# Logits with keys innermost, weighted values with keys outermost, the attention residual put into the accumulation bank, and a written-out instruction sequence

## The chip, the cores and the metric

The kernel runs on one core of one Trainium2 chip. The metric is the time of one execution on the device in microseconds (us), the median of several runs. The core has five engines that run side by side, each through its own list of instructions in order: TensorE (PE; its weight loader is a row of its own, PEld), VectorE (DVE), ScalarE (ACT), GpSimd (POOL) and SyncE (SP), which issues most DMAs. An engine that comes to an instruction whose input isn't there, or whose destination is still in use, waits, and everything behind it in its list waits too. The order of these five lists is therefore a large part of what this kernel is.

## The reference

One block of a transformer on 2048 rows of 640 numbers, in float32: a layer norm, attention in 32 heads of 20 over 8 keys each (the row itself and those 2, 4, ... 14 rows before it), the output projection and a residual; then a second layer norm, a gated feed-forward of width 1728 and a second residual.

```python
q, k, v = heads(layernorm(x) @ wqkv)              # 32 heads of 20
idx = pos[:, None] - 2 * arange(8)                # 8 keys a row, dilation 2
logits = einsum("bhsd,bhswd->bhsw", q, k[idx]) * 20 ** -0.5     # masked where idx < 0
o = einsum("bhsw,bhswd->bhsd", softmax(logits), v[idx])
h = x + o @ wo
n = layernorm(h)
out = h + (silu(n @ w_gate) * (n @ w_up)) @ w_down
```

## The kernel before, in words

**Tiling.** The rows are worked in four batches of 512 (`b`, NB = 4), each as four row blocks of 128 (`j`, NJ = 4). The heads are worked in four groups of eight (`g`, NG = 4, 160 columns). The normalized rows of a batch are turned into columns (transposes L604 for batch 0; by way of VectorE and DRAM for the others) and multiplied with the weights. To keep float32 accuracy each operand is split in two parts (a cast by ScalarE, a subtraction by VectorE), and each product is made of three passes over the parts; so 15 matmuls (three passes, five blocks of 128 columns) make one row block's product. The names are: `x` rows and their columns in `sha` (even batches) or `shb` (odd ones); the K, Q, V weights, loaded at L616 and split at L617 and L619; the products in `bank`s of PSUM (L643), taken out by ScalarE (L648) and stored in DRAM (`ksc`, `qsc`, `vsc`).

**Attention.** For each batch and group, two halves `jp` of two row blocks: VectorE multiplies the query with its eight keys (L692, 2560 elements a partition), sums over the 20 numbers of a head (L699, 128 results), takes the largest over the keys (L706 to L711), ScalarE takes the exponent, VectorE sums (L721), scales, multiplies with the values (L727, 2560) and adds the eight weighted values by halving (L735, L741, and GpSimd in some groups). Within a row block the logits lie key by key, eight heads side by side ("j w h"), and so do the weighted values.

**Output projection** (`wo`, L838). The attention's result comes back in columns (splits L879 and L880), and for each row block `j` and each half of the 640 output columns 15 matmuls of 320 columns accumulate in one bank (L890). ScalarE copies the bank into a scratch row (`XN`, L893), and VectorE adds the scratch row to the residual: in place in the row `h` of batches 1 to 3 (L896, loaded ahead with `x`), or with a freshly loaded row of `x` in batch 0 (L901). Then come the row's statistics (L389 and others), its normalization, the transposes (L504, splits L506 and L507 for a pair of row blocks) and the feed-forward (gates and ups L962, downs L973 and others, with L986 and L990 reading the last gates' banks). The bank of a projection is the next of a list: banks 5, 6 and 7 in batch 0, bank 7 alone in batches 1 and 2, banks 7 and 4 in batch 3. These are the code's numbers; the order shows them as bank_73 to bank_75 for 5 to 7, bank_72 for 4 and bank_68 to bank_71 for 0 to 3.

**What sets the order.** Each piece of work is a call `P.add(engine, cost, function, reads, writes)`. A planner then runs through all of them with a table of costs, several rounds of due times (`ROUNDS`) and a table of corrections (`SHIFT`) to single pieces, and the pieces are issued in the order of the start times so found, as far as what they read and write allows. No bank, row or scratch is chosen by the planner: which bank a piece uses is fixed when it is added.

## Time and profile before

| what | value |
|---|---|
| time of one execution, three runs | 836.17, 837.33, 838.05 us; median 837.33 |
| profiled execution, first to last instruction (its span) | 835.3 us |
| TensorE busy, of the span | 826.3 us (99%) |
| TensorE's weight loader | 712.8 us (85%) |
| VectorE | 755.7 us (90%) |
| ScalarE | 421.3 us (50%) |
| GpSimd | 23.1 us (3%) |
| mean granted clock of TensorE | 0.999 |

The profile gives for the profiled execution its span alone, not a time as the runs have it. The span is 2.0 us under the median of the runs (837.33 - 835.3) and 0.9 under the shortest. In the lines of the profile a row has the engine, the line in the kernel, the operation, what it writes and reads, the shape as partitions x elements, and the times. Where a row ends in a bracket, the bracket tells how long the engine stood idle before it and for what. In the list of waits the three numbers are the sum in us, the count and the longest; in a row of groups they are the sum, the mean of one in ns, and the idle time just before them. A row of stretches has the engines in the order PE, PEld, DVE, ACT, POOL, SP with their busy time, then the granted clock, the busy share of the DMA engines and GB/s.

### The profile page before, as it was taken

To read this page: it belongs to the slowest core of one execution; us is meant where nothing else is said; L and a number is where in the kernel's file an instruction comes from. 1 tells how busy PE (TensorE), PEld (TensorE's weight loads), DVE (VectorE), ACT (ScalarE), POOL (GpSimd) and SP (SyncE) were. 2 spreads that over 40 slices of the span, in tenths; PEclk is the share of its full clock that TensorE was granted. 3 is DMA by queue.
4 is the path that set the end of the run, shared out by engine and by line. 5 is a ranking of instruction groups with operands and counts; after the bars stand their busy time and mean duration, and the time that the engine had idled before them with its cause. 6 is when DMAs were issued, how large, how long until landed. Compare 5 with 4: busy or idle time off the path is not lost.

```text
span 835.3 us, 11299 instructions
## 1 busy us (share of the span) xinstructions
PE 826.3 (99%) x4061; PEld 712.8 (85%) x4061; DVE 755.7 (90%) x916; ACT 421.3 (50%) x740; POOL 23.1 (3%) x34
## 2 busy tenths in 40 slices
PE   8999999999999999999999999999999999999998
PEld 6888888889978888887888888888988888888998
DVE  7599999999999999999999999998869888777982
ACT  7856473333783435654543476565695323323440
POOL 0000000000100000001000000000000000000000
PEclk9999999999999999999999999999999999999999
DMA  8897868568679764899899758899999634457722
GB/s 274 288 348 275 267 213 283 185 207 308 186 219 343 257 197 177 326 303 349 282 313 349 271 173 315 255 288 352 352 339 320 224 115 151 124 175 258 273 99 75
DMA packets 113223, 211.08 MB, mean 253 GB/s; under 512 B 37952, under 2 KB 70400, under 8 KB 112528
## 3 DMA queue, kind: packets, MB, share of 16 engines
q1 hardware_dynamic: 112864, 209.96, 74.0%
q8 instruction: 32, 0.52, 0.2%
q10 hardware_dynamic: 304, 0.41, 0.1%
q14 instruction: 23, 0.19, 0.1%
HBM read 151.27 MB, written 59.05 MB: 252 GB/s over the span
## 4 chain that ended last, share of the span: by engine, by line
PE 84%; DVE 8%; ACT 3%; DMA 3%; issue 1%; SPq 0%; POOL 0%; DVEq 0%; ACTq 0%; POOLq 0%
PE bank L962 22%; PE bank L1046 18%; PE bank L643 15%; PE bank L973 10%; PE bank L1298 7%; PE bank L890 6%; DMA fa<-in_x_dram 2%; PE bank L1103 1%; DVE fa L692 1%; PE bank L1093 1%; DVE fa L735 1%; PE bank L1068 1%; DVE fa L727 1%; DVE fa L699 1%; ACT ra L617 1%
## 5 line engine op out<-in xcount | busy, mean ns | idle before, releaser
L962 PE MATMUL bank<-shb,ra 128*128 128x512 f32 x810 | 190.0, 390 | 1.3 <-DVE shb L507 1.3
L962 PEld LDWEIGHTS bank<-shb,ra 128*128 128x128 f32 x810 | 151.4, 188 | 32.7 <-ACT shb L506 1.5
L643 PE MATMUL bank<-ra,sha 128*128 128x480 f32 x480 | 105.2, 379 | 0.2 <-ACT ra L617 0.2
L643 PE MATMUL bank<-ra,shb 128*128 128x480 f32 x470 | 102.5, 378 | 0.0
L643 PEld LDWEIGHTS bank<-ra,sha 128*128 128x128 f32 x480 | 89.8, 188 | 14.5 <-ACT ra L617 0.6
L643 PEld LDWEIGHTS bank<-ra,shb 128*128 128x128 f32 x470 | 88.1, 188 | 13.2
L692 DVE TENSOR_TENSOR fa<-fa 128x2560 f32<-128x2560 f32 x32 | 90.2, 2820 | 0.9 <-DMA fa<-qsc 0.4
L727 DVE TENSOR_TENSOR fa<-fa 128x2560 f32<-128x2560 f32 x32 | 90.3, 2822 | 0.8
L699 DVE TENSOR_REDUCE fa<-fa 128x128 f32<-128x2560 f32 x32 | 89.9, 2810 | 0.4
L1046 PE MATMUL bank<-shb,ra 128*128 128x512 f32 x360 | 89.4, 395 | 0.6 <-DVE fa L990 0.6
L973 PE MATMUL bank<-ra,acts 128*128 128x512 f32 x328 | 80.7, 391 | 0.0
L1046 PEld LDWEIGHTS bank<-shb,ra 128*128 128x128 f32 x360 | 66.0, 188 | 16.2 <-DVE fa L1223 1.7
L735 DVE TENSOR_TENSOR fa<-fa 128x1280 f32<-128x1280 f32 (+2 forms) x70 | 76.7, 1096 | 1.3
L890 PE MATMUL bank<-ra 128*128 128x320 f32 x480 | 74.1, 310 | 0.0
L890 PEld LDWEIGHTS bank<-ra 128*128 128x128 f32 x480 | 71.7, 188 | 2.4 <-ACT fa L893 1.0
L648 ACT ACTIVATE st<-bank,fa 128x480 f32<-128x480 f32 x64 | 41.0, 656 | 64.1 <-PE bank L643 59.5
L973 PEld LDWEIGHTS bank<-ra,acts 128*128 128x128 f32 x328 | 61.1, 188 | 13.2 <-DVE acts L997 0.5
L1046 PE MATMUL bank<-ra 128*128 128x512 f32 x288 | 69.1, 390 | 0.0
L1046 PEld LDWEIGHTS bank<-ra 128*128 128x128 f32 x288 | 53.9, 188 | 11.1
L1223 DVE TENSOR_TENSOR fa<-bank,fa 128x512 f32<-128x512 f32 x60 | 41.0, 689 | 19.8 <-PE bank L1046 19.0
L939 ACT CAST ra<-fa 128x1280 fp32r<-128x1280 f32 (+1 forms) x38 | 45.6, 1207 | 22.9 <-PE bank L962 12.3
L996 ACT CAST acts<-fa 128x512 fp32r<-128x512 f32 x34 | 21.0, 620 | 48.7 <-DVE fa L986 47.0
(189 smaller groups left out, 1059.8 us busy)
## 6 DMA issues: line engine op xcount, KB each, us to landing
fa<-in_ffn_dram SPq DMA_DIRECT2D x28, 960.0 KB, 6.4
fa<-ksc SPq DMA_DIRECT2D x16, 880.0 KB, 5.4
fa<-vsc SPq DMA_DIRECT2D x16, 880.0 KB, 7.3
ra<-lsc SPq DMA_DIRECT2D x21, 640.0 KB, 5.8
ra<-lsc SPq DMA_DIRECT2D x27, 320.0 KB, 3.7
lsc<-ra SPq DMA_DIRECT2D x13, 640.0 KB, 4.6
fa<-in_ffn_dram SPq DMA_DIRECT2D x12, 640.0 KB, 4.0
ra<-tsc SPq DMA_DIRECT2D x8, 960.0 KB, 7.1
```

The source lines that it names most:

```text
L643: T.matmul(banks[bk][:, 0:480], l, r_(wq(g, w, c), 480), start=(p, c) == first_mm, stop=(p, c) == last_mm)
L648: P.add("ACT", act(480) + 0.06, lambda bk=bk, j=j: A.activation(stage_t()[:, so : so + 1920].rearrange("p (t j c) -> p t j c", t=3, j=NJ)[ ...
L692: P.add("DVE", dve(2560), lambda: V.tensor_tensor(f(PROD, 2560).rearrange("p (j w c) -> p j w c", j=2, w=W), window(ko, 2 * jp), f(qo + 32 ...
L699: P.add("DVE", dve(2560), lambda: V.tensor_reduce(f(lo + 128 * jp, 128), f(PROD, 2560).rearrange("p (n d) -> p n d", d=DH), axis=AX.X, op= ...
L727: V.tensor_tensor(f(PROD, 2560).rearrange("p (j w d) -> p j w d", j=2, d=DH), bass.AP(tensor=fa[:, vo : vo + 160].tensor, offset=fa[:, vo ...
L735: V.tensor_add(dst(v), v[:, :, 0:m, :], v[:, :, m : 2 * m, :])
L890: T.matmul(banks[bk][:, 0:320], l, r_(m, 320), start=p == 0 and c == 0, stop=p == 2 and c == NC - 1)
L939: P.add("ACT", act(n), lambda: A.copy(r_(gu, n), f(raw, n)), r=[rf(raw, n)], w=[rr(gu, n)], prio=PR["fh"])
L962: T.matmul(banks[bk], r_(gu + 1280 * w + wid * c + col, 128), x2(a, c), start=p == 0 and c == 0, stop=p == 2 and c == NC - 1)
L973: T.matmul(banks[bk][:, lo:hi], l, m, start=first and p == 0, stop=last and p == len(passes) - 1)
L1046: T.matmul(banks[bk], r_(ws[w] + 256 * q, 128), x(a, c), start=start and p == n == q == 0, stop=stop and p == 2 and n == len(terms) - 1 an ...
L1298: T.matmul(banks[bks[j]][:, 0:320], t(a, 128, 128 * j), r_(ws[w], 320), start=p == q == 0, stop=p == NP - 1 and q == 2)
```

## The change

It has four parts.

1. The logits lie head by head, the eight keys of a head side by side ("j h w"); the largest and the sum over the keys read eight neighbours. The reduce that makes the logits now writes its 128 results in that order.
2. The weighted values lie key by key across both row blocks of the half ("w n d"), so that each halving is a sum of two stretches without gaps.
3. In batches 1 and 2, and in row blocks 2 and 3 of batch 0, ScalarE copies the residual row into the bank ahead of the output projection's matmuls (20 copies of 320 columns). The first matmul then adds to the bank instead of starting it; ScalarE's copy out of the bank writes the row `h` itself, and VectorE's ten additions (eight of L896, two of L901) are gone. Batch 3 and row blocks 0 and 1 of batch 0 stay as they were.
4. The planner, its costs, `ROUNDS` and `SHIFT` are gone. A table `ORDER` of all pieces, by number, takes their place. The transposes of L504 are issued as matmuls that transpose, in the same number and shape.

```diff
-SHIFT = {
-    7: 3.5, 9: -106.8, 22: 0.4, 31: -515.8, 32: -221.5, 33: -238.8, 34: -84.5, 35: -34.6, 36: -483.8, 37:
...
+ORDER = (
+    10, 9, 0, 2, 31, 32, 6, 11, 1, 34, 22, 23, 24, 7, 12, 13, 33, 14, 19, 20, 8, 36, 21, 16, 39, 37, 38, 118, 17, 18,
...
-                        T.transpose(banks[bk][:, 128 * q : 128 * q + 128], f(XN + 128 * (n0 + q), 128), ident)
+                        T.matmul(banks[bk][:, 128 * q : 128 * q + 128], f(XN + 128 * (n0 + q), 128), ident, is_transpose=True, start=q == 0, stop=q == n - 1, skip_group_check=True)
...
-                f(lo + 128 * jp, 128), f(PROD, 2560).rearrange("p (n d) -> p n d", d=DH), axis=AX.X, op=ALU.add),
+                f(lo + 128 * jp, 128).rearrange("p (j h w) -> p j w h", j=2, h=8), f(PROD, 2560).rearrange("p (j w h d) -> p j w h d", j=2, w=W, d=DH), axis=AX.X, op=ALU.add),
...
-            P.add("DVE", dve(256), lambda: V.tensor_reduce(mx, lg.rearrange("p j w h -> p j h w"), axis=AX.X, op=ALU.max), ...
+            P.add("DVE", dve(256), lambda: V.tensor_reduce(mx, lg, axis=AX.X, op=ALU.max), ...
...
-                        f(PROD, 2560).rearrange("p (j w d) -> p j w d", j=2, d=DH),
+                        f(PROD, 2560).rearrange("p (w n d) -> p n w d", w=W, d=DH),
...
-                    v = f(PROD, 2560).rearrange("p (j w c) -> p j w c", j=2, w=W)
-                    V.tensor_add(dst(v), v[:, :, 0:m, :], v[:, :, m : 2 * m, :])
+                def half(m, dst=PROD):
+                    V.tensor_add(f(dst, 320 * m), f(PROD, 320 * m), f(PROD + 320 * m, 320 * m))
...
+                seeded = b in (1, 2) or (b == 0 and j >= 2)
...
+                    if seeded:
+                        rin, rik = ((lambda o=xr + 320 * half: f(o, 320)), rf(xr + 320 * half, 320)) if b == 0 else hrow(b, j, 320 * half, 320)
+                        P.add("ACT", act(320), lambda bk=bk, rin=rin: A.copy(banks[bk][:, 0:320], rin()), r=[rik], w=[pb(bk)], prio=prio)
...
-                                T.matmul(banks[bk][:, 0:320], l, r_(m, 320), start=p == 0 and c == 0, stop=p == 2 and c == NC - 1)
+                                T.matmul(banks[bk][:, 0:320], l, r_(m, 320), start=not seeded and p == 0 and c == 0, stop=p == 2 and c == NC - 1, skip_group_check=seeded)
...
+                    if seeded:
+                        rout, rok = hrow(b, j, 320 * half, 320)
+                        P.add("ACT", act(320), lambda bk=bk, rout=rout: A.copy(rout(), banks[bk][:, 0:320]), r=[pb(bk)], w=[rok], prio=PR["wev"])
+                        continue
```

The lines of the file move: L604 to L616, L643 to L655, L616 to L628, L504 to L516, L890 to L908, L962 to L983, L990 to L1011, L727 to L739 and so on.

How the new sequence stands against the old one, at the places where the engines wait or are waited for. The first is SyncE's list at the start. Before, the four row blocks of `x` come first (`x` row block 0 as two halves of 64 rows, one of them issued by ScalarE), then the weights:

```order
L572 DMA fa<-in_x_dram 64x640
L577 DMA fa<-in_x_dram 128x1x640 x3
L616 DMA fa<-in_wqkv_dram 128x480 x8
L349 DMA ksc<-fa 8x1120
L349 DMA vsc<-fa 8x1120
L1411 DMA fa<-in_const_dram 128x1x32
L616 DMA fa<-in_wqkv_dram 128x480 x8
L568 DMA fa<-in_x_dram 128x1x2560
L616 DMA fa<-in_wqkv_dram 128x480 x2
```

After:

```order
L584 DMA fa<-in_x_dram 64x640
L628 DMA fa<-in_wqkv_dram 128x480 x4
L589 DMA fa<-in_x_dram 128x1x640 x3
L628 DMA fa<-in_wqkv_dram 128x480 x8
L580 DMA fa<-in_x_dram 128x1x2560
L628 DMA fa<-in_wqkv_dram 128x480 x5
L361 DMA ksc<-fa 8x1120
L361 DMA vsc<-fa 8x1120
L628 DMA fa<-in_wqkv_dram 128x480 x3
```

Four weight blocks now stand between row block 0 and row blocks 1 to 3; the second batch's `x` and all of the first 20 weight blocks stand ahead of row 10, where before the stores of K, Q and V and the loads of `wo` stood between them.

TensorE's list at the start, before (L604 and L616 are transposes, L643 and L655 products of K, Q, V, L554 and L566 fillers):

```order
L554 MATMUL bank_72<-ra 128x512 x10
L604 MATMUL bank_75<-fa 128x128
L604 MATMUL bank_74<-fa 128x128 x8
L554 MATMUL bank_72<-ra 128x512
L604 MATMUL bank_73<-fa 128x128 x3
L604 MATMUL bank_75<-fa 128x128 x4
L643 MATMUL bank_69<-ra,sha_128 128x480
L604 MATMUL bank_74<-fa 128x128 x4
L643 MATMUL bank_69<-ra,sha_128 128x480
```

After:

```order
L616 MATMUL bank_75<-fa 128x128
L616 MATMUL bank_74<-fa 128x128 x4
L655 MATMUL bank_68<-ra,sha_128 128x480 x2
L655 MATMUL bank_68<-ra,sha_129 128x480
L655 MATMUL bank_68<-ra,sha_128 128x480 x2
L655 MATMUL bank_68<-ra,sha_129 128x480
L655 MATMUL bank_68<-ra,sha_128 128x480 x2
L655 MATMUL bank_68<-ra,sha_129 128x480
L655 MATMUL bank_68<-ra,sha_128 128x480
L566 MATMUL bank_72<-ra 128x512
L655 MATMUL bank_68<-ra,sha_128 128x480
L616 MATMUL bank_74<-fa 128x128 x4
```

Before, the transposes of row blocks 0, 1 and most of 2 stand ahead of the first product; now eleven products of row block 0 stand ahead of the second row block's transposes.

TensorE's list from batch 0's output projection (L890, row blocks 2 and 3 in its second part) to the first feed-forward (L962), before:

```order
L643 MATMUL bank_68<-ra,shb 128x480 x15
L643 MATMUL bank_69<-ra,shb 128x480 x15
L890 MATMUL bank_75<-ra 128x320 x15
L890 MATMUL bank_73<-ra 128x320 x15
L890 MATMUL bank_74<-ra 128x320 x15
L890 MATMUL bank_75<-ra 128x320 x15
L643 MATMUL bank_69<-ra,shb 128x480 x15
L643 MATMUL bank_70<-ra,shb 128x480 x15
L643 MATMUL bank_71<-ra 128x480 x5
L643 MATMUL bank_71<-ra,shb 128x480 x5
L643 MATMUL bank_71<-ra 128x480 x5
L504 MATMUL bank_73<-fa 128x128 x2
```

After (L908 and L983 are the same code):

```order
L655 MATMUL bank_70<-ra,shb 128x480 x15
L908 MATMUL bank_75<-ra 128x320 x15
L908 MATMUL bank_74<-ra 128x320 x15
L908 MATMUL bank_73<-ra 128x320 x15
L908 MATMUL bank_75<-ra 128x320 x15
L655 MATMUL bank_68<-ra,shb 128x480 x15
L655 MATMUL bank_69<-ra,shb 128x480 x15
L655 MATMUL bank_71<-ra 128x480 x5
L655 MATMUL bank_71<-ra,shb 128x480 x5
L655 MATMUL bank_71<-ra 128x480 x5
L655 MATMUL bank_70<-ra,shb 128x480 x15
L516 MATMUL bank_73<-fa 128x128 x2
```

Before, five product blocks of the next batch (15 matmuls each) stand ahead of the projection's second part, of which the last two are shown, and three behind it; now four stand ahead, of which the last is shown, and four behind.

VectorE's list near the last gate of a pair of feed-forward blocks, where L990 reads its bank (L1374 adds downs to the row `h`), before:

```order
L1374 TENSOR_TENSOR h_1560<-bank_68,h_1560 128x512
L1374 TENSOR_TENSOR h_1560<-bank_70,h_1560 128x512
L997 TENSOR_TENSOR acts<-fa,acts 128x512
L727 TENSOR_TENSOR fa<-fa 128x2560
L990 TENSOR_TENSOR fa<-bank_73,fa 64x512
L1374 TENSOR_TENSOR h_1560<-bank_69,h_1560 128x512
```

After (L1395 is L1374's code, L1018 L997's, L751 is an addition of the attention's halving, 160 wide):

```order
L1395 TENSOR_TENSOR h_1584<-bank_69,h_1584 128x512
L746 TENSOR_TENSOR fa<-fa 128x640
L751 TENSOR_TENSOR fa<-fa 128x160
L1018 TENSOR_TENSOR acts<-fa,acts 128x512
L751 TENSOR_TENSOR fa<-fa 128x160
L1011 TENSOR_TENSOR fa<-bank_73,fa 64x512
```

Before, a product of 2560 (L727) stands right ahead of L990; now two small pieces and an activation's product (L1018) do.

## The prediction of the time

> **What bounds the kernel now.** I read the page's first part, then who waited for whom on TensorE (PE) and on its weight loader (PEld), then the stretches and the timeline at the places found.
>
> ```profile
> PE 826.3 (99%) x4061; PEld 712.8 (85%) x4061; DVE 755.7 (90%) x916; ACT 421.3 (50%) x740; POOL 23.1 (3%) x34
> ```
> ```profile
> PE bank L604 <- DVE sha L607: 1.4, 1, 1.4
> PE bank L554 <- POOL ra L1401: 1.3, 1, 1.3
> PE bank L962 <- DVE shb L507: 1.3, 1, 1.3
> PE bank L1046 <- DVE fa L990: 0.6, 1, 0.6
> ```
> ```profile
> PEld bank L604 <- DVE sha L607: 1.8, 1, 1.8
> PEld bank L1046 <- DVE fa L1223: 1.7, 6, 0.3
> PEld bank L962 <- ACT shb L506: 1.5, 1, 1.5
> ...
> PEld bank L890 <- ACT fa L893: 1.0, 4, 0.3
> PEld bank L1046 <- DVE fa L990: 1.0, 1, 1.0
> ...
> PEld bank L643 <- ACT ra L617: 0.6, 1, 0.6
> PEld bank L604 <- ACT fa L392: 0.4, 1, 0.4
> PEld bank L604 <- DVE fa L443: 0.4, 1, 0.4
> PEld bank L643 <- DVE ra L619: 0.4, 1, 0.4
> ```
> ```profile
> 820.00:836.00 16.00, 11.45 (x79) 11.19 (x77) 3.23 (x8) 0.00 (x0) 0.00 (x0) 0.92 0.23 83
> ```
>
> TensorE is the bound: 826.3 of 835.3 us. Its matmuls keep their number and shapes, so the change can win only what TensorE stands still: 9.0 us in all. Of these 1.3 lie before its first matmul, and the stretch from 820 has 16.0 - 11.45 = 4.55, of which 0.65 is beyond the span's end, so 3.9 stand behind the last matmul. What is left inside is 3.8 us. A busy row hides the start of a wait, because the last matmul is still on its way through; the loader's rows show the wait fuller (1.8 for 1.4, 1.0 for 0.6). By them the removable waits are: the start 1.8 + 0.4 + 0.4 = 2.6; near 50 us 0.6 + 0.4 = 1.0; before the first feed-forward 1.5; near 566 1.0; behind evictions of the output projection 1.0. That is about 7 us, and the most that any new sequence could take. VectorE (DVE), 90% busy, matters only where TensorE waits for it.
>
> **The change, part by part.**
>
> *Layout of logits and products.* Same counts, and the shapes are as large.
>
> ```profile
> L710 DVE TENSOR_REDUCE fa<-fa 128x32 f32<-128x256 f32 x16 | 10.2, 640 | 0.1
> L706 DVE TENSOR_TENSOR fa<-fa 128x256 f32<-128x256 f32 x4 | 1.6, 412 | 0.1
> L896 DVE TENSOR_TENSOR h<-h,fa 128x640 f32<-128x640 f32 x8 | 6.4, 816 | 0.2 <-ACT fa L893 0.2
> ```
>
> L710 reads 256 elements with keys eight apart and takes 640 ns; L706 reads as many in a row for 412. With keys innermost the reduce should cost about 0.42: 0.22 less. L721 is the same form, so 32 x 0.22 = 7 us less on VectorE (ends 0 and 7.3). The products and halvings (L727, L735) I leave at their price: their runs stay 20 elements or become longer. The logits reduce (L699) now stores its 128 results eight elements apart. At L710's surcharge, 228 ns / 256 = 0.9 ns for each, that is at most 0.11 us in 32 instructions, 3.7 us; I take 0, since one result comes for 20 inputs. The Trainium skill (SBUF — State Buffer, "Door 1: The DMA port swizzle", its note on cachelines) says that lines are 16 bytes and each access that crosses into a new line pays. L710 against L706 agrees, and by that rule the stores would pay too: VectorE would gain 3.5 us here instead of 7. Neither figure enters the sum by itself.
>
> *Residual in the bank.* Ten residual adds of 0.82 (L896, L901) leave VectorE, 8 us. ScalarE gets 20 seeds of 320 elements.
>
> ```profile
> L939 ACT CAST ra<-fa 128x1280 fp32r<-128x1280 f32 x34 | 42.7, 1263 | 21.9 <-PE bank L962 11.3 <-DMA fa<-in_ffn_dram 8.8 <-PE bank L1068 1.7
> L893 ACT COPY fa<-bank 128x320 f32<-128x320 f32 x32 | 13.3, 424 | 27.5 <-PE bank L890 26.5 <-DMA fa<-qsc 0.9
> L940 ACT CAST ra<-fa 128x320 fp32r<-128x320 f32 x6 | 2.7, 458 | 0.3 <-PE bank L1093 0.2
> ```
>
> A copy from SBUF into a bank isn't in the trace; from a bank it takes 424, between SBUF places 458: I take 0.44, 9 us more on an engine that is 50% busy. The Trainium skill (ScalarE: Activation LUTs, "Step-by-step: what each stage is for") calls PSUM the faster destination for ScalarE; by that the seed would be at the lower end, which changes nothing.
>
> The seed is a new wait for TensorE: in batches 1 and 2 all projections use one bank, and between two groups now stand an eviction and a seed.
>
> ```profile
> 307.96 0.86 PE L973 MATMUL bank<-ra,acts 128*128 128x512 f32 x3
> 308.65 2.45 PE L890 MATMUL bank<-ra 128*128 128x320 f32 x15
> 308.16 0.43 ACT L893 COPY fa<-bank 128x320 f32<-128x320 f32 x1 [0.93 <-DMA fa<-qsc]
> ```
>
> Here three matmuls fill 0.69 us between groups, and the eviction (308.16 to 308.59) just held the next group until 308.65. With a seed behind it the filling must be 0.69 + 0.44 = 1.13. In the new row order each gap of batches 1 and 2 has at least five 512-wide matmuls (190.0 / 810 = 0.235 each by the next row, 1.17), and most have more; the seed stands behind its eviction in ScalarE's row. So the four waits of 1.0 roughly stay as others. But in three places a 1280-wide cast (L939, 1.26) stands ahead of an eviction. I take +0.2 (ends -1.0: all gaps are filled; +4: three casts each delay a group by 1.26).
>
> ```profile
> L962 PE MATMUL bank<-shb,ra 128*128 128x512 f32 x810 | 190.0, 390 | 1.3 <-DVE shb L507 1.3
> L643 PE MATMUL bank<-ra,sha 128*128 128x480 f32 x480 | 105.2, 379 | 0.2 <-ACT ra L617 0.2
> ```
>
> *New sequence, the start.* SP now sends four weight loads before rows 1 to 3 of x, and TensorE does some eleven products of the first row block before it transposes the second.
>
> ```profile
> 5.36 0.88 DVE L441 BATCH_NORM_STATS2 fa<-fa 128x6 f32<-128x320 f32 x2
> 8.41 0.66 PE L604 MATMUL bank<-fa 128*128 128x128 f32 x4 [1.40 <-DVE sha L607]
> 10.56 0.47 PE L643 MATMUL bank<-ra,sha 128*128 128x480 f32 x1
> 4.00:5.00 1.00, 1.00 (x4) 0.77 (x3) 0.85 (x4) 0.36 (x2) 0.00 (x0) 1.00 1.00 320
> ```
>
> Four loads of 240 KB at 320 GB/s push x back by 4 x 0.77 = 3.1 us: statistics that began at 5.36 begin near 8.5, the transposes of 8.41 come near 10.4. Until then TensorE, done with the first five transposes near 7, has eleven products (11 x 0.219 = 2.4) and a filler, where it had nothing. Waits remain: a weight split now stands ahead of the piece of row 0 that the first transpose needs (0.35), the cast of its other four pieces (0.5), the fifth weight block, now behind x (0.3), the second row block (0.2): 1.35 for 2.6. Term -1.2; ends -2.2 and, if weights arrive later than so, +0.5.
>
> *Near 50 us.*
>
> ```profile
> 50.15 0.59 ACT L617 CAST ra<-fa 128x480 fp32r<-128x480 f32 x1 [1.17 <-DMA fa<-in_wqkv_dram]
> ```
>
> The last weight block landed late. Now all 20 weight loads are issued before the first K and V stores, ahead of what they queued behind. Term -0.6; ends -1.0 and 0.
>
> *Before the first feed-forward.*
>
> ```profile
> 218.28 8.96 PE L890 MATMUL bank<-ra 128*128 128x320 f32 x60
> 218.59 0.42 DVE L880 TENSOR_TENSOR ra<-fa,ra 128x256 fp32r<-128x256 f32 x1
> 229.51 0.81 DVE L901 TENSOR_TENSOR h<-fa 128x640 f32<-128x640 f32 x1
> 230.36 0.74 ACT L389 ACTIVATE fa<-h 128x640 f32<-128x640 f32 x1 [1.13 <-DVE h L901]
> 239.66 3.68 PE L962 MATMUL bank<-shb,ra 128*128 128x512 f32 x15 [1.26 <-DVE shb L507]
> ```
>
> From the projection's end (227.24) eviction, add, statistics, normalization and columns take 12.4 us to 239.66; TensorE had three blocks of 15 projections (45 x 0.219 = 9.9) and transposes to cover them. Now there are four blocks (13.1), and the add with its queueing, 1.1 us between the eviction and L389, is gone: 11.3 against 13.1 plus transposes. What would be late next is the projection's input, L880, which in the old order ended at 219.0, after the projection began. In VectorE's new row some 8.7 us of attention that stood before it (three 2560-wide instructions) stands behind it, so it can end near 210, and the projection begins near 213 (3.3 by the moved block, 1.8 by the terms above). Term -1.5; ends -1.9 and 0.
>
> *Near 566.*
>
> ```profile
> 562.96 2.81 DVE L727 TENSOR_TENSOR fa<-fa 128x2560 f32<-128x2560 f32 x1
> 565.81 0.69 DVE L990 TENSOR_TENSOR fa<-bank,fa 64x512 f32<-64x512 f32 x1
> ```
>
> TensorE waited for the bank that L990 reads, and L990 stood behind a 2.81 us product. In the new row a 160-wide add and small work stand there. Only ScalarE's activation and L990 itself still lie before the bank. Term -0.6; ends -1.0 and 0.
>
> The six waits on L1223 (1.7) and the tail keep their order in the main; the finer interleaving may cost as much as it saves: 0, ends -0.5 and +1.
>
> Sum: 0.2 - 1.2 - 0.6 - 1.5 - 0.6 + 0 = -3.7. The profiled execution's span is 835.3; its time outside the span isn't shown, and the median, 837.33, is 2.0 above. So 831.6 + 2.0 = 833.6 us.
>
> **Rivals.**
> 1. *The seed chain, slower.* One bank, 16 groups in batches 1 and 2; if ScalarE comes to the eviction behind something that itself waits, each group stands the seed's 0.44 and more. It decides above (3.7 + 1.7) / 16 = 0.34 us a group. If each loses 0.44 beside the sum, 16 x 0.44 = 7.0: 840.6. For it: one bank and in-order ScalarE. Against: ScalarE is half idle and the gaps are filled in the row order. Chance 0.12.
> 2. *Hidden anyway.* TensorE is 99% busy, VectorE's 15 us less are under it, and the late x costs at the start what the other places give, or their waits move to the next late input (weights of the first feed-forward). All waits stay in other places: 837.3. Chance 0.20.
> 3. *All of it.* With VectorE 15 us lighter, every listed wait but the start's 1.0 goes, also half of L1223's: 7 - 1 + 0.8 = 6.8 less: 830.5. Chance 0.10.
>
> **How the numbers follow.** The forecast has 0.58, with its own range 832 to 835.6. Faster by over 0.2% (1.7 us, about what a measurement of this kernel tells from none) are forecast and rival 3: 0.68; within it rival 2: 0.20; slower rival 1: 0.12. The range 831.2 to 837.8 leaves out rival 1, the low part of rival 3 and the upper third of rival 2, about 0.2 in all. It is bounded below by the 7 us of waits.
>
> **What the changed profile would show.** TensorE busy near 826 of a span near 831.6. No wait of over 1 us on L504's successor before the first feed-forward; the one on the last gate's bank under 0.4; two or three waits of about 0.5 in the first 12 us. Reduces over keys near 0.42 us, VectorE near 741 us, ScalarE near 430. Seeds of 0.44. Wrong would be: weight-loader waits behind the seed copies of over 3 us in sum, first products after 8.5 us, or a new wait on feed-forward weights near 240.

## The result: 1.1% slower, with loads that come late

The changed kernel takes 845.75 us (median of four runs, 843.66 to 849.86); the kernel before, timed beside it, 836.99 (836.17 to 838.05). The ratio is 1.011, 95% interval 1.008 to 1.0141. The forecast was 833.6. The profiled execution has a span of 841.9 us and a time of 844.12, one of the two shorter of the four: of the 8.8 us between the medians the traces show 6.6 (841.9 - 835.3).

The first two rows are from the page's first part, before the list of waits of the changed kernel:

```profile
span 841.9 us, 11208 instructions
PE 827.7 (98%) x4061; PEld 712.7 (85%) x4061; DVE 744.6 (88%) x906; ACT 429.1 (51%) x762; POOL 24.6 (3%) x34
```
```profile
PE bank L983 <- ACT ra L960: 2.4, 2, 2.1
...
PE bank L616 <- DVE fa L441: 1.4, 1, 1.4
PE bank L655 <- ACT st L660: 1.4, 1, 1.4
...
PE bank L1067 <- DMA ra<-lsc: 1.0, 1, 1.0
...
PE bank L983 <- ACT shb L518: 0.7, 1, 0.7
...
PEld bank L908 <- ACT bank L901: 0.6, 2, 0.3
```

Three names in these rows are stores in DRAM: `ysc` holds the normalized rows that come back as columns, `osc` the attention's result, `lsc` the split parts of the feed-forward weights.

TensorE does the same work (827.7 us busy against 826.3) and stands 14.2 us instead of 9.0. VectorE is 11 us lighter, as was intended, and it shows nowhere in the time. The weight loader waits for seeds (L901) 0.6 us in all. The largest waits are for weight casts (L960), for an eviction (L660) and for a load (lsc). What these two ScalarE lines themselves wait for is in the same view, first of the kernel after, then of the kernel before (L939 is L960's code, L528 is L540's):

```profile
ACT ra L960 <- DMA fa<-in_ffn_dram: 28.9, 14, 6.2
ACT shb L540 <- DMA fa<-ysc: 15.5, 2, 11.0
```
```profile
ACT ra L939 <- DMA fa<-in_ffn_dram: 8.8, 3, 4.9
ACT shb L528 <- DMA fa<-ysc: 2.2, 2, 1.7
```

ScalarE stands 14 times for feed-forward weights instead of 3, and once for 11.0 us at one load. The timeline shows the two worst places. The first, near 142:

```profile
119.82 0.30 SPq L526 DMA_DIRECT2D ysc<-fa  x1
125.42 0.45 SPq L526 DMA_DIRECT2D ysc<-fa  x1
126.56 1.47 SPq L526 DMA_DIRECT2D ysc<-fa  x2
132.19 0.38 SPq L532 DMA_DIRECT2D fa<-ysc  x1
```
```profile
139.31 0.62 ACT L540 CAST shb<-fa 128x512 fp32r<-128x512 f32 x1 [11.01 <-DMA fa<-ysc]
139.83 0.66 ACT L660 ACTIVATE st<-bank,fa 128x480 f32<-128x480 f32 x1
...
143.93 2.43 PE L655 MATMUL bank<-ra,sha 128*128 128x480 f32 x10 [1.39 <-ACT st L660]
```

Batch 3's turned rows are stored in four DMAs. The first goes at 119.82; SyncE issues other DMAs between it and the rest, so the load that needs all four goes at 132.19, and the cast of what it brings stands at the head of ScalarE's list until 139.31. Evictions of full banks queue behind it: one runs at 139.83, the next at 143.23, behind a table load (1.28) and two more casts, and TensorE runs out of banks. The second place, near 442:

```profile
433.11 0.85 SPq L959 DMA_DIRECT2D fa<-in_ffn_dram  x2
...
443.84 1.26 ACT L960 CAST ra<-fa 128x1280 fp32r<-128x1280 f32 x1 [6.23 <-DMA fa<-in_ffn_dram]
...
445.15 1.43 PE L983 MATMUL bank<-shb,ra 128*128 128x512 f32 x5 [2.05 <-ACT ra L960]
```

A weight load issued at 433.5 is cast at 443.84, and TensorE waits for the cast. Its place was free at 428.3, so it was issued late; but it also flew for 10.3 us, in a stretch in which the DMA engines were busy throughout (share 1.00). The stretch, and the usual flight of such loads before and after:

```profile
433.50:443.80 10.30, 9.60 (x43) 7.62 (x41) 10.06 (x10) 0.60 (x1) 0.00 (x0) 1.00 1.00 346
```
```profile
fa<-in_ffn_dram SPq DMA_DIRECT2D x28, 960.0 KB, 6.4
```
```profile
fa<-in_ffn_dram SPq DMA_DIRECT2D x28, 960.0 KB, 6.7
```

This is general, and the usual flight isn't what changed (6.4 us and 6.7). For each load of feed-forward weights or of their split parts whose landing the trace tells, I took the time from its landing to the first instruction that reads what it brought. The median is 10.1 us before (82 loads) and 5.3 after (73); loads that are read within 0.15 us of landing were 3 and are 12.

The table puts TensorE's stops in order of place: for each pair of neighbouring matmuls the time between their starts beyond the usual spacing of the shape (0.227 us for 512 columns, 0.217 for 480, 0.147 for 320, 0.109 for 128), summed by stretch of the profiled execution. It counts a slow clock too, so a stretch can differ between two executions by 1.6 us without any wait (last section). The runs below the first two are the experiments.

| kernel | 0-20 | 120-160 | 215-245 | 380-470 | 540-600 | rest | sum | span | median time |
|---|---|---|---|---|---|---|---|---|---|
| before | 5.1 | -0.2 | 1.8 | 0.7 | 1.3 | 2.2 | 10.9 | 835.3 | 836.99 |
| after | 6.8 | 1.5 | 0.9 | 3.7 | 3.4 | 0.8 | 17.1 | 841.9 | 845.75 |
| e1 layouts alone | 5.7 | -0.2 | 0.9 | 0.7 | 0.8 | 1.6 | 9.5 | 834.0 | 836.61 |
| e6 old sequence, part seeded | 4.6 | -0.2 | 1.0 | 0.7 | 0.8 | 3.4 | 10.3 | 834.8 | 837.88 |
| e12 two places mended | 5.7 | 4.1 | 1.0 | 2.1 | 3.0 | 1.3 | 17.2 | 841.9 | 843.26 |
| e14 two moves, old sequence | 4.7 | -0.2 | 2.8 | 0.7 | 4.3 | 1.7 | 14.0 | 838.5 | 841.88 |
| e16 half loads | 6.3 | 2.8 | 0.9 | 1.0 | 2.4 | 0.7 | 14.1 | 838.8 | 840.69 |

### The profile page after: what moved, and what is told of

Read it like the earlier page. It is cut to its first block, busy times and chain, and to the rows that moved or that the text cites. A ratio compares the mean times of both kernels' runs of the same rounds, so it can differ in the third digit from the quotient of the medians.

```text
span 841.9 us, 11208 instructions
## 1 busy us (share of the span) xinstructions
PE 827.7 (98%) x4061; PEld 712.7 (85%) x4061; DVE 744.6 (88%) x906; ACT 429.1 (51%) x762; POOL 24.6 (3%) x34
## 4 chain that ended last, share of the span: by engine, by line
PE 67%; DVE 11%; DMA 9%; ACT 7%; SPq 3%; issue 2%; DVEq 0%; ACTq 0%
PE bank L1067 17%; PE bank L983 15%; PE bank L655 10%; PE bank L1319 7%; PE bank L908 7%; PE bank L994 6%; DMA fa<-ysc 3%; DVE fa L739 2%; DMA fa<-in_ffn_dram 2%; DMA ysc<-fa 2%; DVE fa L746 1%; PE bank L1114 1%; PE bank L1089 1%; DVE fa L704 1%; DMA fa<-in_x_dram 1%
## 5 line engine op out<-in xcount | busy, mean ns | idle before, releaser
L983 PE MATMUL bank<-shb,ra 128*128 128x512 f32 x810 | 194.1, 390 | 3.1 <-ACT ra L960 2.4
L983 PEld LDWEIGHTS bank<-shb,ra 128*128 128x128 f32 x810 | 151.0, 188 | 36.0 <-ACT ra L960 3.8
L655 PE MATMUL bank<-ra,sha 128*128 128x480 f32 x480 | 106.9, 382 | 2.1 <-ACT st L660 1.4
L655 PEld LDWEIGHTS bank<-ra,sha 128*128 128x128 f32 x480 | 90.1, 189 | 17.5 <-ACT sha L618 2.0
L655 PE MATMUL bank<-ra,shb 128*128 128x480 f32 x470 | 102.5, 378 | 0.0
L655 PEld LDWEIGHTS bank<-ra,shb 128*128 128x128 f32 x470 | 88.1, 188 | 13.2
L1067 PE MATMUL bank<-shb,ra 128*128 128x512 f32 x360 | 90.1, 393 | 1.0 <-DMA ra<-lsc 1.0
L739 DVE TENSOR_TENSOR fa<-fa 128x2560 f32<-128x2560 f32 x32 | 90.3, 2822 | 0.9
L994 PE MATMUL bank<-ra,acts 128*128 128x512 f32 x328 | 84.3, 390 | 0.0
L908 PE MATMUL bank<-ra 128*128 128x320 f32 x480 | 74.4, 309 | 0.0
L908 PEld LDWEIGHTS bank<-ra 128*128 128x128 f32 x480 | 71.9, 188 | 2.3 <-ACT bank L901 0.6
L660 ACT ACTIVATE st<-bank,fa 128x480 f32<-128x480 f32 x64 | 40.4, 657 | 48.2 <-PE bank L655 36.1
L960 ACT CAST ra<-fa 128x1280 fp32r<-128x1280 f32 (+1 forms) x38 | 45.8, 1206 | 29.6 <-DMA fa<-in_ffn_dram 28.9
L1226 ACT CAST ra<-fa 128x512 fp32r<-128x512 f32 x30 | 18.0, 618 | 46.9 <-PE bank L1067 23.8
```

Of the source, the lines that this page charges most:

```text
L655: T.matmul(banks[bk][:, 0:480], l, r_(wq(g, w, c), 480), start=(p, c) == first_mm, stop=(p, c) == last_mm)
L739: V.tensor_tensor(f(PROD, 2560).rearrange("p (w n d) -> p n w d", w=W, d=DH), bass.AP(tensor=fa[:, vo : vo + 160].tensor, offset=fa[:, vo ...
L908: T.matmul(banks[bk][:, 0:320], l, r_(m, 320), start=not seeded and p == 0 and c == 0, stop=p == 2 and c == NC - 1, skip_group_check=seeded)
L960: P.add("ACT", act(n), lambda: A.copy(r_(gu, n), f(raw, n)), r=[rf(raw, n)], w=[rr(gu, n)], prio=PR["fh"])
L983: T.matmul(banks[bk], r_(gu + 1280 * w + wid * c + col, 128), x2(a, c), start=p == 0 and c == 0, stop=p == 2 and c == NC - 1)
L994: T.matmul(banks[bk][:, lo:hi], l, m, start=first and p == 0, stop=last and p == len(passes) - 1)
```

## The experiments

They were timed in groups, each beside the kernel before, whose median was 836.6 to 837.5 in them; so the times of two groups are compared by their ratios, or to about 1 us.

In kernels whose table of places is shorter by two lines, the profile's lines are two lower: L958 is L960's code, L899 L901's, L906 L908's, L653 L655's.

**Which part costs the time: layouts, seeds or sequence.** The layouts alone, in the kernel before:

```diff
-                f(lo + 128 * jp, 128), f(PROD, 2560).rearrange("p (n d) -> p n d", d=DH), axis=AX.X, op=ALU.add),
+                f(lo + 128 * jp, 128).rearrange("p (j h w) -> p j w h", j=2, h=8), f(PROD, 2560).rearrange("p (j w h d) -> p j w h d", j=2, w=W, d=DH), axis=AX.X, op=ALU.add),
...
```

> The kernel before with the two new layouts alone (logits with keys innermost, weighted values with keys outermost); planner, residual adds and sequence as before. Theory A (the new sequence costs the time, by lists that stand at loads which come late): VectorE about 7 us less busy (32 reduces over 256 elements at 0.41 instead of 0.635), TensorE's waits as before, so the time is 836 to 837.5. Theory B (the seeded bank costs it): the same, 836 to 837.5. Theory C (the new layouts cost it, by something the row of busy times doesn't show): 840 or more.

Measured (e1): 836.61, ratio 0.9994 (0.9986 to 1.0003). The groups of this run show the reduces at 0.41 and 0.40 us (0.64 and 0.63 before), and the store into places eight apart at no price (2.813 us against 2.810):

```profile
L699 DVE TENSOR_REDUCE fa<-fa 128x128 f32<-128x2560 f32 x32 | 90.0, 2813 | 0.4
L710 DVE TENSOR_REDUCE fa<-fa 128x32 f32<-128x256 f32 x16 | 6.6, 410 | 0.1
L721 DVE TENSOR_REDUCE fa<-fa 128x32 f32<-128x256 f32 x16 | 6.4, 399 | 0.2 <-ACT fa L712 0.2
```

7.3 us less in these reduces, and 6.1 less on VectorE in all (749.6 against 755.7), are worth nothing in time: theory C falls.

All edits in the old sequence, that is, the changed kernel with another table:

```diff
-    10, 9, 0, 2, 31, 32, 6, 11, 1, 34, 22, 23, 24, 7, 12, 13, 33, 14, 19, 20, 8, 36, 21, 16, 39, 37, 38, 118, 17, 18,
+    9, 0, 6, 10, 15, 1, 3, 11, 29, 28, 2, 31, 32, 33, 34, 35, 12, 16, 19, 22, 43, 25, 7, 8, 36, 37, 39, 38, 40, 41, 44,
...
```

The table is the order of the kernel before, with each seed right behind the eviction of the group before it in its bank.

> All edits of the change, but every engine's list in the order of the kernel before; the 20 seeds stand right behind the eviction of the same bank, or shortly ahead of the first group. Theory A (the sequence costs the time): 834.5 to 837.5, with seeds that cost at most 1 us of waits. Theory B (a seed between two groups of one bank holds TensorE): 841 to 846, with waits of TensorE's weight loader behind the seed of 4 us or more in sum.

Measured (e2): 851.95, ratio 1.0171 (1.0158 to 1.0184), outside what A expected and above B. B's sign came too, since the weight loader waits 15.8 us behind seeds; but 9.1 of them are a single wait, and it isn't B's chain of many small ones. The waits of this run:

```profile
PE bank L906 <- ACT bank L899: 11.8, 6, 8.7
...
ACT bank L899 <- DMA h<-in_x_dram: 11.6, 1, 11.6
```

One seed, the first of batch 2, waits for its residual, and TensorE 8.7 us for it; of the other five waits one is 1.7, at batch 0's seeds, and four are 0.34. A residual that was needed behind the projection is now needed ahead of it. In this run the store that empties its place is issued at 459.6 us, the load goes at 466.2 and lands at 472.1, and TensorE was ready for the projection at 463.9. So batch 2 was seeded in its last two row blocks alone, and batch 0's seeds were put earlier:

```diff
-                seeded = b in (1, 2) or (b == 0 and j >= 2)
+                seeded = b == 1 or (b in (0, 2) and j >= 2)
```

> All edits and the old sequence, like the run with all seeds, but batch 2 is seeded in row blocks 2 and 3 alone (its residual can't be loaded before the row's place is free, and the first two row blocks are projected sooner), and batch 0's seeds stand earlier in ScalarE's list. Sum from the run with all seeds: 849.7 - 8.7 (the wait for batch 2's residual) - 1.7 (batch 0's seeds) = 839.3 of span, and some of the 0.34 us waits behind seeds fewer: 840 to 841.5 as time. If seeds cost nothing where the residual is there: 836 to 838.5. If the one-bank chain holds TensorE also then: 843 or more.

Measured (e6): 837.88, ratio 1.0012 (1.0003 to 1.0022): the case that seeds cost next to nothing where the residual is there. TensorE waited 0.7 us for them:

```profile
PE bank L906 <- ACT bank L899: 0.7, 2, 0.3
```

Four of the 20 seeds are missing here, and in the changed kernel all 20 cost the loader 0.6. With e1 this leaves the sequence. Undoing the seeds in it doesn't help:

```diff
-                seeded = b in (1, 2) or (b == 0 and j >= 2)
+                seeded = False
```

> The new sequence and layouts, but without the seeds: evictions go to the scratch row again and VectorE adds the residual (ten adds, each behind the second eviction of its row block). Theory A: 843 to 847, the waits of the changed kernel at the start, at 142, 442 and 571 us are all there. Theory B: 836 to 839.

Measured (e3): 865.69, ratio 1.0331 (1.0307 to 1.0354). That is worse than either theory: the ten adds, each behind its second eviction, delay normalizations (stops of 5.4 us at 215-245 and 8.0 in 245-380), and the waits of the changed kernel at the start, near 142 and in 380-470 are there too; that at 571 isn't. So the run says little of the seeds: where these adds stand, the new sequence has no room for them, and no other places were tried.

**Is it the start?** One move in VectorE's list:

```diff
-    10, 9, 0, 2, 31, 32, 6, 11, 1, 34, 22, 23, 24, 7, 12, 13, 33, 14, 19, 20, 8, 36, 21, 16, 39, 37, 38, 118, 17, 18,
+    10, 9, 0, 2, 31, 32, 6, 11, 1, 34, 33, 22, 23, 24, 7, 12, 13, 14, 19, 20, 8, 36, 21, 16, 39, 37, 38, 118, 17, 18,
```

> The changed kernel with one move in VectorE's list at the start: the 128 columns of the first normalized row block that the first transpose reads are made ahead of the first split of a weight block, which waits for the weight's load. If that split is what holds the first transpose (it began at 7.33 us, and at 5.74 before): first transpose near 5.7, and 1 to 1.6 us less in all, 842.2 to 843. If the products behind it wait for the weights anyway: first transpose near 5.7, first product still near 8.3, and the time within 0.4 us of the changed kernel.

Measured (e4): 845.65, ratio 1.0102 (1.0072 to 1.0132). The first transpose moved from 7.33 to 5.65, the first product from 8.34 to 7.40, and the stops of the first 20 us stayed at 6.7. In part the next late input took the place (the first product waited 1.01 for a cast of its columns, L616); in part the clock did, which was 0.50 from 8.9 to 12.2 in this execution. The whole old start (first 100 pieces in the old order, the rest as in the changed kernel), VectorE's first rows:

```diff
 L435 TENSOR_REDUCE fa<-fa 128x1
 L436 TENSOR_SCALAR fa<-fa 128x1
-L354 MEMSET fa 128x1
+L439 TENSOR_SCALAR fa<-fa 128x128
 L439 TENSOR_SCALAR fa<-fa 128x512
-L629 TENSOR_TENSOR ra<-fa,ra 128x480
-L439 TENSOR_SCALAR fa<-fa 128x128
-L629 TENSOR_TENSOR ra<-fa,ra 128x480 x2
+L451 BN_STATS fa<-fa 128x6 x2
...
```

> The changed kernel with the first 100 pieces in the old order (all of x ahead of the weights, transposes of three row blocks ahead of the first product), the rest as in the changed kernel. Theory A2: the start's stops fall from 6.7 us to 5.2 to 5.7, so 844.3 to 844.8 against 845.7 of the changed kernel; the other stops stay. If the start decided more than its own stops: 842 or less.

Measured (e8): 847.48, ratio 1.0134 (1.0105 to 1.0163), not to be told from the changed kernel. The sum for the start is 6.8 here as well, where 5.2 to 5.7 was expected. The waits did go back to the old ones (1.41 us at 8.41, 1.40 in the kernel before), but the clock differs, first here, then in the kernel before:

```profile
10.70:14.00 3.30, 3.30 (x12) 2.85 (x11) 3.30 (x8) 3.30 (x10) 0.00 (x0) 0.50 0.91 297
```
```profile
10.70:14.00 3.30, 3.30 (x19) 2.93 (x19) 3.30 (x8) 3.30 (x11) 0.00 (x0) 1.00 0.82 270
```

The matmuls of this stretch stand 1.6 us further apart than usual; without that the start has 5.2. The start isn't where the 9 us are: it gives 1.7 at most.

**Are late loads enough to make it slow?** (Theory A2, here and above: the new sequence issues loads with too little lead, and ScalarE's list, and so TensorE, stands at them.) In the old sequence (layouts, no seeds) each feed-forward weight load was put 5 us later in SyncE's list, as far as its use allows; the first of them in SyncE's list:

```diff
-L957 DMA fa<-in_ffn_dram 128x1920 x2
 L883 DMA fa<-osc 128x2x256 x2
+L957 DMA fa<-in_ffn_dram 128x1920
 L692 DMA fa<-ksc 128x1x1760
+L957 DMA fa<-in_ffn_dram 128x1920
...
```

> The kernel before with the new layouts and without seeds (as the layout run, 836.6), but with SyncE's list so that each feed-forward weight load is put 5 us later, as far as its first use allows. Theory A2: 840 to 846, with new waits of ScalarE at the weight casts of 10 us or more and new stops of TensorE in batches 0 to 2. If a shorter lead is harmless in the old sequence: 836 to 838.

Measured (e7): 863.48, ratio 1.0305 (1.027 to 1.0339), more than expected. ScalarE's group of casts shows it (8.8 us of waiting before):

```profile
L958 ACT CAST ra<-fa 128x1280 fp32r<-128x1280 f32 x34 | 42.9, 1263 | 59.6 <-DMA fa<-in_ffn_dram 50.5 <-PE bank L981 8.4 <-PE bank L1065 0.8
```

**Can the new sequence be mended by putting loads ahead?** Three reorderings of whole lists. First, 49 loads go ahead by up to seven places, for example:

```diff
 L664 DMA vsc<-st 64x2x640
-L664 DMA vsc<-st 64x2x640
 L530 DMA fa<-ysc 128x5x512
+L664 DMA vsc<-st 64x2x640
...
```

> The changed kernel; only SyncE's list is reordered: 49 loads behind which an engine stood with less than 4 us to spare go up to 7 places ahead, as far as the place they fill is free by then. Theory A2 (the new sequence issues loads with too little lead, and ScalarE's list and so TensorE stand at them): 837.5 to 841.5, ScalarE's waits at the feed-forward weight casts fall from 28.9 us to under 15, and the stops of TensorE at 442 and 571 us are gone. Theory D (the DMA engines themselves are short of time there, so that a load put ahead only pushes another back): 844 to 848, with the same sum of stops in other places.

Measured (e5): 855.77, ratio 1.0219 (1.0202 to 1.0237), slower than either theory. The casts wait 23.2 us instead of 28.9, but what was pushed back, above all the stores and loads of the attention's result, is now late (10.4 us of waits at the projection's casts). Then SyncE's list, ScalarE's list and both in the order in which the pieces were ready. SyncE's list at its first change, and ScalarE's:

```diff
 L626 DMA fa<-in_wqkv_dram 128x480
+L1430 DMA fa<-in_const_dram 128x1x32
 L626 DMA fa<-in_wqkv_dram 128x480
...
```
```diff
 L627 CAST ra<-fa 128x480
+L441 ACTIVATE fa<-fa 128x640
 L627 CAST ra<-fa 128x480
...
-L441 ACTIVATE fa<-fa 128x640
+L407 ACTIVATE fa<-fa 128x640
 L616 CAST sha<-bank 128x512
...
```

> The changed kernel; SyncE's list alone is put in the order in which its DMAs were ready (data there, place free) in the trace of the changed kernel. In that trace SyncE stood idle for 510.8 us, 453.3 of them with a later DMA of its list ready; in the kernel before 529.3 and 233.9. Theory A3 (loads are late because SyncE's list stands at an entry that isn't ready while loads behind it are): 838 to 842, weight loads land with 8 us or more to spare at the median (5.3 in the changed kernel, 10.1 before). Theory D (the DMA engines are short of time): 844 to 850, spare time as before.

> The changed kernel; ScalarE's list alone is changed: where it stood at an entry that wasn't ready, pieces behind it that were ready go ahead (199 pieces; pieces that need a table of functions keep their order among themselves). If ScalarE's list is the way by which late loads reach TensorE: 839 to 843, the stop at 142 us, behind a cast that waited 11 us for its load, is gone. If the late loads reach TensorE by their own data: 844 to 847.

> Both of these in one kernel. If the lists' standing is the cause (A3): 836.5 to 840, and as good as the kernel before. If something else of the sequence (VectorE's or TensorE's order) costs the time: over 842.

Measured (e9, e10, e11): 876.79 (ratio 1.0485, 1.046 to 1.051), 873.66 (1.0453, 1.044 to 1.0467) and 893.34 (1.0693, 1.0655 to 1.0731). All far slower, against A3. In the first the feed-forward loads do land with 10.5 us to spare at the median, as in the kernel before, and yet the waits of that run are:

```profile
ACT shb L538 <- DMA fa<-ysc: 27.7, 2, 16.2
...
ACT ra L887 <- DMA fa<-osc: 22.1, 6, 5.4
...
PE bank L653 <- ACT st L658: 11.9, 3, 9.5
```

So it isn't how long a list stands at an entry while others are ready, nor the lead of the usual load. As I read these waits, what counts is that the few transfers on which TensorE's next block hangs are early, and a list by readiness puts others ahead of them; no run shows this by itself.

**Two places mended alone.** SyncE's list, the two moves:

```diff
 L526 DMA ysc<-fa 32x20x128
+L526 DMA ysc<-fa 32x20x128 x3
 L666 DMA ksc<-st 64x2x640
...
-L526 DMA ysc<-fa 32x20x128
...
-L526 DMA ysc<-fa 32x20x128 x2
...
+L959 DMA fa<-in_ffn_dram 128x1920
 L1349 DMA out_dram<-h
...
-L959 DMA fa<-in_ffn_dram 128x1920
```

> The changed kernel with two moves in SyncE's list and nothing else: the four stores of batch 3's turned rows (issued at 119.8, 125.4, 126.6 and 127.4 us between eleven other DMAs) follow each other, so that the load behind them and the casts at 139.3 come about 6 us sooner; and the feed-forward weight load whose place was free at 428.3 and which was issued at 433.5 goes ahead of five entries. If the stops at 142 (1.6 us) and 442 us (2.3) come from these places in the list: both go, the profiled span is 838 to 839, the time 841.5 to 842.5. If they only move to the next late load: the sum of TensorE's stops stays near 17 us and the time at 844 to 847.

Measured (e12): 843.26, ratio 1.0077 (1.0058 to 1.0095), between the two expectations and 2.5 us less than the changed kernel by the medians. The stops at 142 and 442 are gone, and in the profiled run others of the same sum stand for them: evictions wait for a store that the four now delay (125 us), and a weight cast at 413. The sum, 17.2, has 1.6 of slow clock behind the stop at 125.

```profile
PE bank L653 <- ACT st L658: 2.4, 1, 2.4
...
PE bank L981 <- ACT ra L958: 1.4, 1, 1.4
```

The places were real, but they weren't single.

**Taking away what the late loads need.** Each feed-forward weight load brings half its columns and leaves the other half out; no list is touched.

```diff
-            P.add("SP", 0.45, lambda: Q.dma_start(f(raw, n + m), src), w=[rf(raw, n + m)], prio=PR["fld"], nbytes=nb(128, 4 * (n + m)))
+            P.add("SP", 0.45, lambda: Q.dma_start(f(raw, (n + m) // 2), src[:, : (n + m) // 2]), w=[rf(raw, n + m)], prio=PR["fld"], nbytes=nb(128, 4 * (n + m)))
```

> The changed kernel, lists untouched, but each feed-forward weight load fetches the first half of its columns alone (480 KB for 960; the other half of the weights is what stood there), so that it lands sooner and leaves the DMA engines to the others. If the time is lost because loads issued late land late: the casts that wait for these loads (28.9 us of ScalarE's waits in the changed kernel) wait under 15, stops of TensorE between 380 and 600 us at most half of their 6.9, time 838.5 to 842.5. If the lists' order itself holds the engines, whatever the loads take: 843.5 to 847.

> The control: the old sequence with the new layouts and without seeds (836.6 as it is), with the same half loads (the other half of the weights is what stood there). Its loads land 10 us ahead at the median, so 836.0 to 837.0. If a load's flight still decides something here: 835.5 or less.

Measured: 840.69 in the new sequence (e16; ratio 1.005, 1.0036 to 1.0064), 5.1 us under the changed kernel by the medians and 3.1 by the profiled spans; 836.06 in the old (e17; 0.999, 0.998 to 1.0), by its ratio no faster than e1 (0.9994). The casts' waiting falls to 11.6 us (28.9 before the halving), and the stops of 380-470 from 3.7 to 1.0:

```profile
L960 ACT CAST ra<-fa 128x1280 fp32r<-128x1280 f32 (+1 forms) x38 | 45.6, 1204 | 12.5 <-DMA fa<-in_ffn_dram 11.6 <-PE bank L983 0.7
```

This is the clearest run: the same lists, sooner landings, and about half of the loss is back (5.1 of 8.8 by the medians, 3.1 of 6.6 by the spans), while the old sequence hardly notices. The half loads take both away, time of flight and traffic on the DMA engines, so the run doesn't tell late issue from crowded DMA engines (theory D). What remains, 4.6 us between the two (840.69 - 836.06), is by the table the turned rows near 142 (2.8 in this run), the start and 540-600; no run removes these.

**The prediction's two places by themselves.** Old sequence, layouts, no seeds; TensorE's list, then VectorE's near 566:

```diff
-L653 MATMUL bank_69<-ra,shb 128x480 x15
 L906 MATMUL bank_75<-ra 128x320 x15
 L906 MATMUL bank_73<-ra 128x320 x15
 L906 MATMUL bank_74<-ra 128x320 x15
 L906 MATMUL bank_75<-ra 128x320 x15
-L653 MATMUL bank_69<-ra,shb 128x480 x15
+L653 MATMUL bank_69<-ra,shb 128x480 x30
...
-L737 TENSOR_TENSOR fa<-fa 128x16x8x20
+L1393 TENSOR_TENSOR h_1560<-bank_69,h_1560 128x512
 L1009 TENSOR_TENSOR fa<-bank_73,fa 64x512
-L1393 TENSOR_TENSOR h_1560<-bank_69,h_1560 128x512
+L737 TENSOR_TENSOR fa<-fa 128x16x8x20
```

> The old sequence with the new layouts and without seeds (836.6 in its own run) and two moves: batch 0's projection of row blocks 2 and 3 stands one product block earlier (its input's cast and split go ahead of two normalizations and one attention product), and the subtraction that frees the last gate's bank near 566 stands ahead of the attention product. If the prediction's steps for these two places are right by themselves: 0.5 to 1.0 us less in front of the first feed-forward and 0.5 near 566, 835.0 to 836.0. If both waits only move to the next late piece: 836.3 to 837.2. If what is delayed by them is missed: 838 or more.

Measured (e14): 841.88, ratio 1.0059 (1.0046 to 1.0072): what is delayed was missed. Near 566 the timeline shows the product (L737) in front of the next thing TensorE needs, where before it stood in front of the bank:

```profile
565.16 0.69 DVE L1009 TENSOR_TENSOR fa<-bank,fa 64x512 f32<-64x512 f32 x1 [2.06 <-ACT fa L1008]
565.89 2.83 DVE L737 TENSOR_TENSOR fa<-fa 128x2560 f32<-128x2560 f32 x1
...
569.35 0.69 DVE L1011 TENSOR_TENSOR acts<-fa,acts 64x512 fp32r<-64x512 f32 x1
...
570.09 1.28 PE L1122 MATMUL bank<-ra,acts 128*128 128x320 f32 x6 [2.07 <-DVE acts L1011]
```

## Why the prediction was wrong, step by step

The sum was -3.7 from 835.3 of span; the profile has +6.6, a miss of 10.3.

- *The layouts*: right in size (reduces at 0.41 against 0.42 forecast, 32 of them) and right in that they don't enter the sum; VectorE as a whole became 11.1 us lighter, not 15. The rule of the Trainium skill (SBUF — State Buffer, "Door 1: The DMA port swizzle", on lines of 16 bytes) would have had the scattered stores pay; 2.813 against 2.810 us says that they don't here. That the 20 inputs of each result hide them is an argument, not shown.
- *The seeds*, +0.2: right. A seed takes 0.427 us (0.44 forecast), the loader waited 0.6 for them in all. What the step left out is the residual's new due time: the seed needs it ahead of the projection. The new sequence provides for it, with 0.6 of waits; e2 shows what it costs where nothing does (8.7 us).
- *The start*, -1.2: wrong, +1.7 (5.1 to 6.8). The step priced the weight split ahead of the first row's piece at 0.35. It put the first transpose back by 1.6 (7.33 against 5.74), since the split waits for a cast that waits for the weight:

```profile
5.71 0.59 ACT L629 CAST ra<-fa 128x480 fp32r<-128x480 f32 x1 [1.42 <-DMA fa<-in_wqkv_dram]
6.33 0.66 DVE L631 TENSOR_TENSOR ra<-fa,ra 128x480 fp32r<-128x480 f32 x1 [1.14 <-ACT ra L629]
6.91 0.28 DVE L441 TENSOR_SCALAR fa<-fa 128x128 f32<-128x128 f32 x1
...
7.33 1.30 PE L616 MATMUL bank<-fa 128*128 128x128 f32 x5 [1.39 <-DVE fa L441]
```

  The duration of an instruction was taken for the time that it holds its list. This isn't the whole of the 1.7, since e4 took the wait away without a gain in time. Products still started at least 0.40 us apart up to 10.7 us here (usual 0.217), four of them, so by an estimate some 0.7 is slow clock; how much of that the new order brings about is open.
- *Near 50*, -0.6: the stop is gone, but e1 lost it too, with the old order of the weight loads. So the moved loads aren't shown to be what did it; with one trace of the kernel before it may have been an accident of one execution.
- *Before the first feed-forward*, -1.5: measured -0.9, and e1 has the same 0.9 in the old sequence. So the moved block isn't needed for it; moved by itself (e14) the place has 2.8.
- *Near 566*, -0.6: the wait for L990's bank is gone, but the stretch 540-600 rose from 1.3 to 3.4. Its largest wait is now for a load of split weights that landed late:

```profile
572.29 2.11 PE L1067 MATMUL bank<-shb,ra 128*128 128x512 f32 x8 [1.01 <-DMA ra<-lsc]
```

- *All the rest*, 0 with ends -0.5 and +1: this is the step that failed. The prediction followed the waits that were there and asked of each whether it goes; it didn't ask of the loads that were covered whether they still are. Stretches that had no stop to speak of, 120-160 and 380-470, gained 1.7 and 3.0 us; with 540-600, where 2.7 more stand than the step for 566 allowed (+2.1 against -0.6), that is 7.4 us for a term of 0 with an end of +1. The start's 2.9 (+1.7 against -1.2) is the next largest share of the miss. The prediction had the rows of SyncE's list in hand (415 rows became 467: runs of equal DMAs were broken up), and never set the issue of a feed-forward load against its use. The kernel before issued these loads 0.1 us after their place was free at the median, the changed one 1.5 (136 loads of weights and split parts each, by the last use or landing that the trace tells).

Of the rivals, the first had the side right and the mechanism wrong: no chain of seeds, but lists that stand at loads. The range's upper end, 837.8, took the bounds of the listed terms and had none for waits that didn't exist yet. The same holds for the signs that it named, none of which came: the loader waited 0.6 behind seeds and not 3, the first product began at 8.34 and not after 8.5, and the stop near 240 (0.73) was for a cast of columns, not for weights.

What is shown: the sequence costs the time (e1, e6), and about half of it is back when the feed-forward loads are smaller (e16). That the other half has the same cause is read from the waits alone. What stays open: why the new sequence has these loads late, how much of it is late issue and how much crowded DMA engines, and whether a few more moves would mend it. Mended at two places it came to 843.26; nothing here beat the kernel before by more than the measurement can tell (e1, 0.9994).

## What to carry to other kernels

When a change replaces the whole order, list the transfers that are hidden today, with the time from landing to first use, and see where the new order puts their issue: on an engine that is 99% busy every gain is bounded by the waits that exist, and the losses are bounded by nothing. An in-order list that stands at one late load holds everything behind it, so the price of a moved entry is the time that its input is late, not its duration. And a wait that goes in a run that doesn't touch its cause is no safe term of a sum.

## What the runs showed of the hardware that was not expected

After a stop of a little over 2 us TensorE's clock fell to half in several runs, for 3.41 us each time. The stretches below are of the run with two places mended (after a stop of 2.37 us at 125) and of the run with two moves (2.07 us at 568); the number behind the brackets of POOL is the granted clock:

```profile
127.50:132.00 4.50, 4.33 (x13) 3.66 (x14) 4.40 (x4) 3.65 (x9) 0.00 (x0) 0.62 0.90 267
```
```profile
570.00:574.20 4.20, 4.11 (x18) 4.11 (x19) 4.07 (x8) 2.00 (x4) 0.00 (x0) 0.61 0.97 330
```

The mean over these 4.50 and 4.20 us is 0.62 and 0.61; within them the clock is 0.50 from 128.6 to 132.0 and from 570.9 to 574.3. That cost another 1.6 us each time: eight matmuls 0.183 over their usual spacing, thirteen 0.12. The length of the stop alone doesn't decide: the stop of 2.05 us at 442 in the changed kernel cost none (clock 1.00 from 445.2 to 449.0), and neither did one of 2.65 us that ended at 144.7 in the run with half loads:

```profile
144.50:149.00 4.50, 4.28 (x20) 3.74 (x21) 4.50 (x4) 2.51 (x6) 0.00 (x0) 1.00 1.02 287
```

Longer stops had stretches of twice and three times 3.41 us at half, as the 8.7 us stop of e2 (10.2 us). The Trainium skill (TensorE: Matmul & The Clock Gate, "What's actually happening") has the gate close after an idle window of about 3.4 us; here 2.1 was once enough. The clock also fits the wide spread of the changed kernel's runs: those at 843.66 and 844.12 had a mean clock of 0.999, those at 847.38 and 849.86 had 0.996 and 0.994. One stretch of 3.41 us at half lowers the mean over 842 us by 0.002, so by an estimate these two had one or two and two or three of them; they were not traced.
